# An SSM–MLP forward-and-gradient kernel: main part fused in 512-token chunks, operands turned on chip, up-projections in halves

## The chip, the cores and the metric

The kernel runs on one core of a Trainium2 chip. The metric is device time in microseconds (us), lower is better; several executions are taken of each kernel, and each execution is marked fast or slow. Comparisons are made between fast ones. Engines are named as in the profile: PE multiplies matrices (PEld loads its stationary operand), DVE works on vectors, ACT evaluates functions and scales, POOL and SP mostly issue transfers in this kernel.

## The reference, cut to what matters

Two long-convolution layers alternate with two MLPs, and everything is differentiated:

```python
x = A_q                                     # 2048 tokens x 448, bf16
x = x + A(layernorm(x))                     # A(n) = n * y,  y = fftconv(shift(k) * v, ssm_k) + D * kv
x = x + silu(layernorm(x) @ w1) @ w2        # 448 -> 1792 -> 448
x = x + A(layernorm(x))                     # the same y
x = x + silu(layernorm(x) @ w1) @ w2
out, vjp = jax.vjp(...)                     # 9 outputs: out and the gradients of
                                            # q, k, v, shift_k, ssm_k, D, w1, w2
```

`y` is the same for both layers. So the work falls into a **prefix** (FFT convolution that makes `y`), a **main part** (four residual blocks forward, four backward) and a **suffix** (FFT work of the gradients of k, v, ssm_k). The weight gradients are 896 matmuls that contract over all 2048 tokens; each group of them needs the activations or the up-gradients of a whole layer.

## The kernel before

The main part is a sequence of stages over all tokens. Cuts and shortened lines are marked by dots.

```python
def _forward(k):
    ...                                     # shift product for all 16 token tiles
    _b_forward(k, 0, ...)                   # MLP 0, four chunks of 512 tokens
    for g in range(4): ...                  # layernorm and shift product, all tokens
    _b_forward(k, 1, ...)                   # MLP 1
    for ft in range(NF): ...                # w1 and w2 transposed on PE (112 transposes)

def _b_forward(k, L, ...):
    for c in range(4):
        n_g = _ln_group(...)                # layernorm of this chunk, then 16 transposes
        for fp in range(NF // 2):           # 7 x 8 matmuls, 512 columns
            ...                             # ps_f -> silu, tanh on ACT -> three DVE instructions
        ...                                 # store aT and dT to DRAM
        for tl in range(4): ...             # down-projection, 14 matmuls each, X += ps_o

def _backward(k):
    _b_backward(k, 1, ...); _a_backward(k, 2, ...)
    _b_backward(k, 0, ...); _a_backward(k, 0, ...)   # each _a_backward tile feeds 14 weight-gradient matmuls

class _JFeed:                               # the feeder; one weight-gradient group, cut:
    ...
    nc.sync.dma_start_transpose(out=st[:], in_=stat_d[ft, :, :])     # 512 KB, turned while loading
    for t in range(NT):
        nc.tensor.matmul(ps[:, :D], lhsT=st[:, t, :], rhs=mov[:, t, :], ...)
```

The backward product through w2 contracts 448 rows as four blocks of 112 (`w2T[DC, ND, F]`, DC = 112).

## Time and profile before

| what | value |
|---|---|
| time | 1066.78 us median (1057.07 to 1072.07, 4 runs) |
| PE / DVE / ACT busy in the profiled run (span 1068.9 us) | 808.4 / 653.9 / 391.1 us |
| mean granted PE clock | 0.894 |
| prefix / main / suffix | 176 / 614 / 279 us |

The three parts are read off the table by stage, which the prediction shows. A row has the window, then busy time (and number of instructions) of PE, PEld, DVE, ACT, POOL, the granted clock, the busy share of the 16 transfer engines and GB/s. No engine is full; each stage has another one near its limit, and holes lie at the borders.

### The profile page before, as it was taken

How to read it: one execution, taken by the hardware profiler on the slowest of the kernel's cores; microseconds unless marked ns; L12 is line 12 of the kernel's file. 1: busy time of each engine (PE TensorE's matmuls, PEld its weight loads, DVE VectorE, ACT ScalarE, POOL GpSimd, SP SyncE). 2: the span in 40 equal slices, each digit the busy share in tenths (PEclk: the TensorE clock that was granted, in tenths of full speed). 3: DMA queues.
4: the chain of work that ended last, by engine and by line, in shares of the span. 5: the costliest groups of instructions: out<-in, count | busy, mean ns of one | idle time of the engine just before them, and what ended most of it. 6: DMA issues, size and time to landing. Idle time of an engine off the chain costs nothing.

```text
span 1068.9 us, 12750 instructions
## 1 busy us (share of the span) xinstructions
PE 808.4 (76%) x4908; PEld 429.4 (40%) x4908; DVE 653.9 (61%) x1174; ACT 391.1 (37%) x531; POOL 120.7 (11%) x175
## 2 busy tenths in 40 slices
PE   0676724999699985999977988984737977688387
PEld 0344402444344443444433433431314654445173
DVE  4887738787975562476777866785534663334144
ACT  1768615666566551111233400121213442313112
POOL 1002102111321110000011100010100000102112
PEclk9989976999899995999999989997768988779699
DMA  8516761444436556846799934669789699769945
GB/s 312 196 65 246 237 176 53 168 155 155 172 138 195 179 163 58 230 165 203 240 273 243 251 118 153 218 171 188 148 229 199 184 226 248 226 169 234 163 127 135
DMA packets 173866, 198.00 MB, mean 185 GB/s; under 512 B 121952, under 2 KB 143712, under 8 KB 172525
## 3 DMA queue, kind: packets, MB, share of 16 engines
q1 hardware_dynamic: 151678, 106.56, 41.2%
q0 software_dynamic: 21248, 87.65, 25.0%
q10 hardware_dynamic: 878, 2.98, 0.8%
q8 instruction: 38, 0.62, 0.2%
q14 instruction: 24, 0.19, 0.1%
HBM read 82.59 MB, written 84.87 MB: 157 GB/s over the span
## 4 chain that ended last, share of the span: by engine, by line
issue 43%; PE 15%; POOL 4%; DMA 3%; DVE 2%; ACT 1%; POOLq 0%; DVEq 0%; ACTq 0%
PE ps_f L537 3%; PE ps_d L738 3%; PE ps_o L555 3%; PE ps_b L630 2%; DMA GH_d<-ghT 1%; PE ps_gK L856 1%; DMA out_dram<-dout 1%; PE ps_w2t L512 1%; POOL GH_d L633 1%; POOL W1TP_d L696 1%; PE ps_w1t L505 1%; DMA out_dram<-gk 1%; DMA dstat<-GH_d 1%; POOL W2P_d L696 1%; POOL out_dram L709 1%
## 5 line engine op out<-in xcount | busy, mean ns | idle before, releaser
L738 PE MATMUL ps_d<-dmov,dstat 128*128 128x448 bf16 x896 | 210.5, 387 | 54.9 <-DMA dstat<-GH_d 30.6
L738 PEld LDWEIGHTS <-dstat 128*128 128x128 bf16 x896 | 91.6, 106 | 150.2 <-issue 37.9
L630 PE MATMUL ps_b<-gT,w2T 112*128 112x512 bf16 x448 | 108.4, 389 | 12.0 <-DVE ghT L631 11.9
L537 PE MATMUL ps_f<-nT,w1sb 112*128 112x512 bf16 x448 | 108.9, 391 | 9.5 <-DVE nT L114 8.4
L631 DVE SCALAR_TENSOR_TENSOR ghT<-dTl,ps_b 128x512 bf16<-128x512 bf16 x112 | 75.9, 685 | 37.0 <-PE ps_b L630 26.5
L555 PE MATMUL ps_o<-w2sb,aT 128*128 128x448 bf16 x448 | 91.5, 353 | 1.0 <-ACT aT L539 1.0
L639 PE MATMUL ps_n<-w1T,ghT 128*128 128x448 bf16 x448 | 88.8, 354 | 0.0
L568 DVE SCALAR_TENSOR_TENSOR lb_junk<-lb_u,nch 128x448 bf16<-128x448 f32 x64 | 39.8, 622 | 66.1 <-ACT lb_u L565 66.0
L565 ACT ACTIVATE lb_u<-ps_n,rhalf 128x448 f32<-128x448 f32 x32 | 20.3, 635 | 163.2 <-issue 125.3
L630 PEld LDWEIGHTS <-w2T 112*128 112x128 bf16 x448 | 44.2, 99 | 71.2 <-issue 27.5
L537 PEld LDWEIGHTS <-w1sb 112*128 112x128 bf16 x448 | 44.5, 100 | 67.3 <-issue 23.3
L539 ACT ACTIVATE aT<-ps_f 128x1024 bf16<-128x1024 f32 x56 | 58.1, 1038 | 11.6 <-PE ps_f L537 7.5
L272 PE MATMUL ps_v<-Gsb,pa 128*128 128x128 bf16 x336 | 48.0, 231 | 18.6 <-DVE pa L812 16.0
L639 PEld LDWEIGHTS <-ghT 128*128 128x128 bf16 x448 | 44.0, 98 | 42.6 <-issue 1.1
L555 PEld LDWEIGHTS <-aT 128*128 128x128 bf16 x448 | 42.5, 98 | 46.1 <-ACT aT L539 6.7
L541 ACT ACTIVATE tm<-ps_f 128x1024 bf16<-128x1024 f32 x56 | 58.2, 1040 | 0.0
L447 ACT ACTIVATE n_g<-X,ln_nmr,rstd 128x448 bf16<-128x448 f32 x41 | 30.1, 770 | 67.1 <-DVE ln_nmr L441 43.8
L112 ACT COPY dpart<-ps_d 128x448 f32<-128x448 f32 x28 | 14.9, 532 | 97.4 <-PE ps_d L738 90.1
L273 PE MATMUL ps_v<-Gsb,pb 128*128 128x128 bf16 x336 | 44.8, 232 | 5.2 <-DVE pb L406 4.6
L272 PEld LDWEIGHTS <-pa 128*128 128x128 bf16 x336 | 34.9, 104 | 25.5 <-DVE pa L812 19.7
L572 DVE SCALAR_TENSOR_TENSOR lb_v<-nch,lb_cc,lb_u 128x448 f32<-128x448 bf16 x64 | 43.6, 682 | 1.0
L525 PE MATMUL ps_nt<-ident,n_g 128*112 128x128 bf16 x128 | 12.2, 245 | 40.8 <-ACT n_g L447 40.8
(173 smaller groups left out, 1244.2 us busy)
## 6 DMA issues: line engine op xcount, KB each, us to landing
A_d<-aT POOLq DMA_DIRECT2D x8, 1792.0 KB, 8.2
DT_d<-dT POOLq DMA_DIRECT2D x8, 1792.0 KB, 10.3
dTl<-DT_d SPq DMA_DIRECT2D x8, 1792.0 KB, 12.8
GH_d<-ghT POOLq DMA_DIRECT2D x8, 1792.0 KB, 12.7
N_d<-n_g POOLq DMA_DIRECT2D x16, 448.0 KB, 3.8
nch<-N_d SPq DMA_DIRECT2D x16, 448.0 KB, 5.0
spec_K<-Ka POOLq DMA_DIRECT2D x2, 1792.0 KB, 7.8
kbc<-spec_K SPq DMA_DIRECT2D x14, 256.0 KB, 5.1
```

Source lines behind the costliest of these rows:

```text
L272: nc.tensor.matmul(pv[:, i, :], lhsT=pa[:, i * P:(i + 1) * P], rhs=k.Gsb[:, ga, :], start=True, stop=False)
L273: nc.tensor.matmul(pv[:, i, :], lhsT=pb[:, i * P:(i + 1) * P], rhs=k.Gsb[:, gb, :], start=False, stop=True)
L537: nc.tensor.matmul(ps[:, u, :], lhsT=w1sb[:, dc, ft * P:(ft + 1) * P], rhs=nT[:, dc, :], start=(dc == 0), stop=(dc == ND - 1))
L539: nc.scalar.activation(asl, ps[:], ACT.Silu)
L541: nc.scalar.activation(tm[:], ps[:], ACT.Tanh, scale=-0.5)
L555: nc.tensor.matmul(po[:, :D], lhsT=aT[:, ft, tl * P:(tl + 1) * P], rhs=w2sb[:, ft, :], start=(ft == 0), stop=(ft == NF - 1))
L568: nc.vector.scalar_tensor_tensor(out=junk[:], in0=u0[:], scalar=1.0, in1=n_t, op0=ALU.mult, op1=ALU.mult, accum_out=cpair[:, 1:2])
L572: nc.vector.scalar_tensor_tensor(out=v[:], in0=n_t, scalar=cc[:, 1:2], in1=u0[:], op0=ALU.mult, op1=ALU.add)
L630: nc.tensor.matmul(ps[:], lhsT=w2T[:, dc, ft * P:(ft + 1) * P], rhs=gT[:, dc, :], start=(dc == 0), stop=(dc == ND - 1))
L631: nc.vector.scalar_tensor_tensor(out=ghT[:, ft, :], in0=dT[:, ft, :], scalar=1.0, in1=ps[:], op0=ALU.add, op1=ALU.mult)
L639: nc.tensor.matmul(pn[:, :D], lhsT=ghT[:, ft, tl * P:(tl + 1) * P], rhs=w1T[:, ft, :], start=(ft == 0), stop=(ft == NF - 1))
L738: nc.tensor.matmul(ps[:, :D], lhsT=st[:, t, :], rhs=mov[:, t, :], start=(t == 0), stop=(t == NT - 1))
```

## The change

Its intent is to overlap the stages. A chunk of 512 tokens goes through shift, layernorm, MLP and, in layer 1, backward at once, while the next chunk's shift and layernorm are prepared; the up-projection is written in two halves so that one half of the next chunk comes between. Further parts: constants come ready as bf16; the shift convolution moves from DVE to PE; weight-gradient operands are turned by a transfer from SBUF to SBUF and stored turned; w1 and w2 are transposed by transfers. The suffix swaps one spectrum instead of two, and the feeder is gone: the weight gradients are low-priority instructions that the scheduler places. The diff is cut to its core; dots mark cuts and shortened arguments.

```diff
-    k.A_d = [... [NF, P, S] ...]             # loads turn
+    k.A_d = [... [P, NF, NT, P] ...]         # stored turned
+    def store_turned(self, dst, tile_, c, hh):
+        an = self.td.tile([P, NF // 2, 4, P], BF16, name="turned", tag="S", bufs=2)
+        nc.sync.dma_start_transpose(out=an, in_=tile_)
+        nc.gpsimd.dma_start(out=dst[:, 7 * hh:7 * hh + 7, 4 * c:4 * c + 4, :], in_=an[:])
...
+    def run(self):
+        for c in range(4):                                  # layer 0 forward
+            ...a_fwd(c + 1), nb = b_pre(c + 1)              # next chunk's shift, layernorms
+            self.h(c, 0, nT, 1, cur)                        # second half of this up-projection
+            nT = self.b_tr(nb)
+            self.h((c + 1) % 4, 0 if c < 3 else 1, nT, 0, fol)   # first half of the next
+            self.out(c, cur, False)
+        for c in range(4):                                  # layer 1, forward and backward
+            gb, gT = self.g_pre(c, 1)
+            self.h(c, 1, nT, 1, cur)
+            na1, nb1 = self.a_fwd(c + 1, 2, None), self.b_pre(c + 1, 3)
+            self.out(c, cur, True)
+            ghT = self.ga(c, 1, gT, cur)
+            nT = self.b_tr(nb1); self.h(c + 1, 1, nT, 0, cur)
+            self.gn(c, 1, ghT, nb, ...)
+        for c in range(4):                                  # layer 0 backward
+            ghT = self.ga(c, 0, gT, dT); ...; self.gn(c, 0, ghT, nb, ...)
...
-    nc.tensor.matmul(ps[:], lhsT=w2T[:, dc, ...], rhs=gT[:, dc, :], ...)          # 4 blocks of 112 rows
+    r0 = 64 if b == 3 else 0
+    nc.tensor.matmul(ps[:, u, :], lhsT=self.w2T[r0:P, b, ...], rhs=gT[r0:P, b, :], ...)   # 128, 128, 128, 64
```

## The prediction

> **What bounds the kernel now.** I read the engine totals first, then the 40 slices, the busy time stage by stage, the costliest groups, and last the DMA issues of one line.
>
> No engine is full over the run: PE 808.4 us of 1068.9 (76%), DVE 653.9 (61%), ACT 391.1 (37%). The slices show why:
>
> ```profile
> PE   0676724999699985999977988984737977688387
> ...
> DVE  4887738787975562476777866785534663334144
> ...
> PEclk9989976999899995999999989997768988779699
> ```
>
> PE is at 9 only where an MLP runs, and DVE is low exactly there. The table by stage (window, then busy time and instructions of each engine, granted clock, DMA share, GB/s) makes it exact:
>
> ```profile
> 0.00:25.00 25.00, 0.13 (x2) 0.13 (x3) 11.54 (x13) 3.18 (x2) 3.76 (x11) 1.00 0.87 313
> 25.00:104.00 79.00, 53.23 (x418) 32.49 (x418) 65.24 (x102) 57.93 (x69) 9.11 (x13) 0.96 0.47 172
> ...
> 141.00:176.00 35.00, 2.77 (x17) 2.03 (x18) 20.80 (x37) 4.05 (x7) 2.59 (x3) 0.56 0.50 151
> 176.00:280.00 104.00, 98.67 (x496) 46.30 (x494) 83.11 (x159) 69.30 (x80) 17.63 (x19) 0.98 0.42 145
> 280.00:302.00 22.00, 11.89 (x50) 5.80 (x51) 19.83 (x59) 12.93 (x17) 8.62 (x8) 0.69 0.51 183
> 302.00:396.00 94.00, 90.16 (x468) 43.13 (x467) 59.77 (x101) 55.30 (x60) 11.64 (x14) 1.00 0.53 167
> 396.00:433.00 37.00, 21.53 (x140) 14.93 (x140) 7.39 (x21) 5.80 (x11) 0.51 (x1) 0.54 0.75 128
> ...
> 710.00:790.00 80.00, 46.43 (x177) 20.02 (x177) 43.34 (x79) 14.92 (x38) 8.11 (x15) 0.79 0.80 168
> 790.00:844.00 54.00, 37.84 (x242) 20.53 (x243) 21.77 (x28) 14.33 (x15) 3.24 (x6) 0.81 0.81 204
> ```
>
> Three gaps: nothing on PE before 24.9 us; 35 us at 141 with PE at 2.77 (the first shift and layernorm, for all tokens, before any MLP); 37 us at 396 with DVE at 7.4 (weights being transposed). The first `ps_f` starts at 176 us, the suffix at about 790. So I split the run as **prefix 176, main 614, suffix 279**.
>
> Groups (busy, mean ns, idle before and what ended it):
>
> ```profile
> L738 PE MATMUL ps_d<-dmov,dstat 128*128 128x448 bf16 x896 | 210.5, 387 | 54.9 <-DMA dstat<-GH_d 30.6
> L568 DVE SCALAR_TENSOR_TENSOR lb_junk<-lb_u,nch 128x448 bf16<-128x448 f32 x64 | 39.8, 622 | 66.1 <-ACT lb_u L565 66.0
> L525 PE MATMUL ps_nt<-ident,n_g 128*112 128x128 bf16 x128 | 12.2, 245 | 40.8 <-ACT n_g L447 40.8
> ```
>
> The weight gradients (`ps_d`) wait for their transposed operand, the layernorm backward on DVE waits for ACT, and a new MLP's transposes wait for layernorm: all stage boundaries. Mean ns of pipelined matmuls overlap; by their starts, fed ones come 55 to 56 ns apart at 128 columns, 189 to 192 at 448 and 220 to 227 at 512. The transposing loads hold the SP queue:
>
> ```profile
> L734 SPq DMA_TRANSPOSE dstat<-A_d x28: 1318/4154/9980, 395.2 to 910.3; - x28
> ```
>
> (minimum/median/maximum ns; those of `GH_d` have median 2642.) A plain load's issue takes SP 300 to 600 ns.
>
> **What the Trainium skill says.**
> - "TensorE: Matmul & The Clock Gate", Part 2, Back-to-back issue gap: about N/2.4 + 2.5 ns when warm, 56 for 128 columns, 216 for 512. The trace agrees (55 to 56; 220 to 227).
> - "VectorE: DVE Perf Modes", The TRN2 errata, and Why PSUM operands drop a tier: fp32 and PSUM operands go one element a cycle, (N+151)/0.96 ns. 448 gives 624; the trace's `lb_junk` has 622. bf16 two-operand work runs at twice that; 1024 gives 690, the trace 685.
> - "Advanced Engine Details and Errata", X-Bar Transpose (TRN2): transpose DMAs are as fast as regular ones. The trace agrees for landing (512 KB in 6.3 us median, plain ones 4.7 to 5.8), not for the issuing queue, which is held for microseconds.
> - "Perfetto Trace Analysis", Optimization Strategy: interleave stages whose most contended engines differ. The table above is such a case: 302:396 is PE, 280:302 DVE.
>
> **The change part by part.** Little arithmetic goes away, so I price stages.
>
> *Floor.* PE's work in the changed kernel (its instruction order has as many rows, 9626 against 9818), at fed spacings, is about 713 us. ACT rises to about 436 us (391 before), DVE is about 639 (654 before). The gain must come from overlap.
>
> *Prefix.* bf16 constants and a stored inverse matrix take the casts and 64 transposes off the start: I put the first PE work at about 7 us instead of 24.9. The shift convolution leaves DVE (28 ops of 128x1792, 35 us) for 256 matmuls of 112 columns, 256 x 0.056 = 14 us. The spectra product is software-pipelined. The step to inverse output (`ps_y`) ended at 141; less 18 for the start and some 15 of the 35 us (the rest lay beside ACT's casts) gives about 107. Then only chunk 0 has to be shifted and normalised, about 10 us instead of 35. First up-projection at **117** (176 before): 59 gained.
>
> *Main.* DVE per 512-token chunk, by durations of before's rows:
> - Up-projection: 7 pairs x (0.44 + 0.69 + 0.69) = 12.75 (silu and its derivative). Residual 4 x 0.616 = 2.5. Two layernorms 2 x 4 x (0.60 + 0.17), with small ops 6.8. Shift products 3.1. Layer 0 forward: **25.1**.
> - Fused layer 1 adds `ghT` 7 x 1.22 = 8.5 (from PSUM), eight layernorm backwards at .622 + .082 + .165 + .682 + .681 = 2.23 = 17.9, and gradient products 5.0: **56.5**.
> - Layer 0 backward: 8.5 + 17.9 + 7.4 = **33.8**.
>
> Four of each: 100 + 226 + 135 = **461 us on DVE**. PE per chunk forward: 56 up-projection matmuls x 0.222 = 12.4, 56 down x 0.191 = 10.7, 16 transposes x 0.056 = 0.9, 24 in all; backward has the same counts (`ps_b`, `ps_n`); a fused chunk has both, 48. Four of each: 4 x 96 = **386 us**, and 227 `ps_d` x 0.19 = 43 more that main still holds (below): 429. I checked the forward figure: the last forward chunks of before come every 25.2 us. DVE therefore becomes the bound of main, where before PE was (302:396: PE 90 of 94). The order also shows only 227 of 896 `ps_d` before the end of main, against about 453 before. DVE runs in order and per token tile waits for ACT's scaled copy of PSUM about 0.35 to 0.4 us, x64 = 24, and there are chunk ends: I add 7%. Main **about 490** (614 before).
>
> *Moved with it.* 24 turns on chip (128x3584, 917 KB) take the place of 42 of the 56 transposing loads. They sit on SP, beside work, two per half chunk. The 112 PE transposes of w1 and w2 go, and with them the 37 us hole at 396. One partial sum (`W1TP`) stored and reloaded goes too.
>
> *Suffix.* Now 669 `ps_d` are left instead of 443. Terms: gY's first stages and turns 22; product of 7 pairs at about 10.3 = 72 (PE: before's 844:934 took 90 for it, at DMA share 1.01, now without the swapped loads); gK 14, gkv 10, shift-kernel gradient 12, gk about 14; the last 448 `ps_d` alone, 448 x 0.195 = 88; stores 6. Sum **238** (279 before). The 226 more matmuls cost 43 us; dropped transposes, wide instead of narrow matmuls and relieved transfers pay for them.
>
> Sum: 117 + 490 + 238 = **845**; I say **850**, as waits are more often forgotten than invented.
>
> **The rivals.**
> - *The SP queue bounds main.* A turned tile is 1.75 times a loaded one; scaling the held times of 2.6 to 4.15 us by that gives an estimated 5 to 7 us and perhaps 9. A fused chunk has four: 20 to 36 us of 57. For it: other loads and stores on that queue stand behind, only three buffers hold operands. Against: it fits the chunk. If each turned tile held up its next user, +20 us a fused chunk: 930.
> - *DVE's waits are not hidden.* Its chain per token tile is serial with ACT's, and `lb_junk` already waited 66 us. If main stays 20% over its DVE work: 555, total 910.
> - *The end is a tail of weight gradients on PE alone.* Counted above. If it is fed slowly (each group of 32 needs two or more 512 KB operands; 6.3 us landings, DMA share already 1.05 in before's 975:1018) it takes 110 rather than 88: 870.
> - *Everything overlaps.* Prefix 110, main 477, suffix 225: 812.
>
> **Range and chances.** Best case 812, less some error in the suffix: 800. A bad one is half of one of the first two rivals plus the slow tail, 910. To be within 2% of 1065 it would have to lose every gain but 21 us, which needs two rivals in full together. Faster 0.97, within 2% 0.02, slower 0.01.
>
> **What would show it.** Right: first PE work near 7 us, first up-projection (`ps_h`) near 117; main ending near 605; DVE over 85% busy in the fused layer-1 stretch with PE near 80%; a solid stretch of the last 448 `ps_d` with PE at 9 and DVE almost idle, about 88 us; no slice of clock near 0.55 in the middle. Wrong: transposes in the SP queue holding it over 7 us, with PE or DVE groups waiting for turned operands (first rival); DVE under 80% in that stretch and `lb_junk` again waiting for ACT (second); `ps_d` waiting for DMA at the end (third). The prediction is wrong altogether if main does not drop below 540, or if the prefix still reaches 140.

## The result, and the profile after

The changed kernel takes **879.88 us** (median; 874.28 to 890.23, 4 runs, one of them slow; 878.35 is the median of the fast ones) against 1066.78 before. The ratio is 0.8239, 95% interval 0.8153 to 0.8325. PE is busy for 776.9 of 879.5 us (88%), DVE for 582.2, ACT for 390.4. The slices of the changed kernel's page:

```profile
PE   6888699689999999999998988888788995989997
...
DVE  4498877588866979979698987882474743650100
...
PEclk9899889989999999999999999998899997999999
```

PE works from the first slice, no slice of clock near 0.55 is left, and DVE is busy beside PE up to slice 27. The last four slices are PE alone. The table by stage of the changed kernel, cut at the first `ps_h`, the first `ps_g` (backward of layer 1), the start of layer 0's backward, the end of the main part, the end of the spectra product, and the end of the k gradient:

```profile
0.00:109.00 109.00, 83.98 (x915) 63.04 (x921) 77.60 (x140) 73.38 (x88) 28.10 (x54) 0.95 0.97 277
109.00:251.00 142.00, 128.67 (x639) 60.02 (x639) 111.09 (x253) 103.98 (x132) 31.61 (x39) 0.94 0.94 243
251.00:443.00 192.00, 182.41 (x898) 78.44 (x907) 155.89 (x315) 93.49 (x139) 22.94 (x29) 1.00 0.71 188
443.00:604.00 161.00, 144.47 (x673) 60.50 (x680) 133.48 (x271) 39.92 (x93) 17.86 (x26) 0.97 0.64 208
604.00:713.00 109.00, 91.03 (x815) 58.51 (x821) 58.41 (x83) 49.93 (x52) 9.67 (x17) 0.94 0.81 256
713.00:790.00 77.00, 62.27 (x380) 36.00 (x379) 37.12 (x93) 20.71 (x24) 17.99 (x31) 0.89 0.84 223
790.00:880.00 90.00, 84.04 (x472) 42.95 (x469) 8.61 (x14) 8.99 (x15) 10.48 (x15) 0.98 0.64 155
```

So prefix, main part and suffix are 109, 495 and 275 us, against 176, 614 and 279. **Of the 190 us between these two profiled runs, 67 are won in front and 119 in the main part; the suffix as a whole gave 4.** The group that the prediction led with, and the transposing transfers (the turned tile and the remaining turning loads; minimum/median/maximum ns on SP):

```profile
L731 PE MATMUL ps_d<-dmov,dstat 128*128 128x448 bf16 x896 | 190.9, 359 | 16.1 <-DMA dstat<-A_d 13.1
...
L473 SPq DMA_TRANSPOSE turned<-aT x16: 4107/4278/7912, 120.9 to 405.8; - x16
...
L711 SPq DMA_TRANSPOSE dstat<-GH_d x14: 1322/1934/10212, 724.2 to 860.8; - x14
```

`ps_d` waits 16.1 us instead of 54.9. A turn of 917 KB holds SP for 4.28 us, less than the 5 to 7 estimated.

### The profile page after: what moved, and what is told of

The parts are those of the page before. It is cut to its first block, busy times and chain, and to the rows that moved or that the text cites. A ratio compares the mean times of both kernels' runs of the same rounds, so it can differ in the third digit from the quotient of the medians.

```text
span 879.5 us, 12450 instructions
## 1 busy us (share of the span) xinstructions
PE 776.9 (88%) x4783; PEld 399.5 (45%) x4812; DVE 582.2 (66%) x1166; ACT 390.4 (44%) x539; POOL 138.7 (16%) x209
## 4 chain that ended last, share of the span: by engine, by line
issue 43%; DVE 13%; DMA 8%; PE 7%; POOL 6%; ACT 3%; POOLq 0%; DVEq 0%; ACTq 0%; SPq 0%
PE ps_g L582 4%; DMA turned<-ghT 3%; DMA turned<-aT 3%; PE ps_o L551 2%; DMA out_dram<-gK 2%; DVE w1p L537 2%; DVE dT L538 2%; DVE X L603 1%; DVE lb_junk L599 1%; DVE lb_u L602 1%; DVE w1p L536 1%; POOL out_dram L768 1%; PE ps_h L528 1%; POOL W2P_d L741 1%; POOL GH_d L593 1%
## 5 line engine op out<-in xcount | busy, mean ns | idle before, releaser
L731 PE MATMUL ps_d<-dmov,dstat 128*128 128x448 bf16 x896 | 190.9, 359 | 16.1 <-DMA dstat<-A_d 13.1
L582 PE MATMUL ps_g<-gT,w2T 128*128 128x512 bf16 (+1 forms) x430 | 120.3, 383 | 3.4 <-DVE ghT L585 1.9
L528 PE MATMUL ps_h<-nT,w1sb 112*128 112x512 bf16 x448 | 108.8, 391 | 7.4 <-ACT dT L533 6.0
L582 PEld LDWEIGHTS <-w2T 128*128 128x128 bf16 x448 | 36.0, 96 | 87.0 <-issue 67.3
L532 ACT ACTIVATE aT<-ps_h 128x1024 bf16<-128x1024 f32 (+1 forms) x64 | 59.0, 922 | 17.8 <-issue 9.5
L533 ACT ACTIVATE dT<-ps_h 128x1024 bf16<-128x1024 f32 (+1 forms) x64 | 59.2, 925 | 0.0
L585 DVE SCALAR_TENSOR_TENSOR ghT<-dT,ps_g 128x1024 bf16<-128x1024 bf16 (+1 forms) x32 | 34.2, 1078 | 11.7 <-PE ps_g L582 11.5
L537 DVE TENSOR_TENSOR w1p<-w1p,aT 128x1024 bf16<-128x1024 bf16 (+1 forms) x64 | 39.6, 618 | 0.9
L538 DVE TENSOR_TENSOR dT<-w1p,dT 128x1024 bf16<-128x1024 bf16 (+1 forms) x64 | 39.5, 617 | 0.8
L238 PEld LDWEIGHTS <-pb 128*128 128x128 bf16 x336 | 33.1, 100 | 13.2 <-DVE pb L826 4.6
L585 DVE SCALAR_TENSOR_TENSOR ghT<-dTl,ps_g 128x1024 bf16<-128x1024 bf16 (+1 forms) x32 | 34.6, 1082 | 5.0 <-PE ps_g L582 5.0
```

Source lines behind the costliest of these rows:

```text
L238: nc.tensor.matmul(pv[:, i, :], lhsT=pb[:, i * P:(i + 1) * P], rhs=k.Gsb[:, gb, :], start=False, stop=True)
L528: nc.tensor.matmul(ps[:, u, :], lhsT=self.w1sb[:, dc, ft * P:(ft + 1) * P], rhs=nT[:DC, dc, :], start=(dc == 0), stop=(dc == ND - 1))
L532: nc.scalar.activation(a, ps[:, 0:n, :], ACT.Silu)
L533: nc.scalar.activation(tm, ps[:, 0:n, :], ACT.Tanh, scale=-0.5)
L537: nc.vector.tensor_tensor(out=wv, in0=wv, in1=a, op=ALU.mult)
L538: nc.vector.tensor_tensor(out=tm, in0=wv, in1=tm, op=ALU.subtract)
```

## The experiments

Every kernel below is the changed kernel with the edit shown. All gave right results except the one that is wrong on purpose. Medians are of all runs; slow runs are in four of them (one each of changed, no_wgrad and full_rows, two of wgrad_main_64). Differences are between medians of the fast runs alone, against 878.35. The ratios to the kernel before, taken on the same chip, are the check.

| kernel | median us | difference | ratio to before, 95% interval |
|---|---|---|---|
| changed | 879.88 | | 0.8239 (0.8153 to 0.8325) |
| chunk_by_chunk | 1007.97 | +130 | 0.9467 (0.9398 to 0.9535) |
| whole_up | 923.34 | +45 | 0.8655 (0.8587 to 0.8722) |
| shift_all_first | 912.13 | +34 | 0.8544 (0.8492 to 0.8597) |
| turn_on_load | 900.74 | +22 | 0.8479 (0.8427 to 0.8532) |
| dve_extra | 891.46 | +13 | 0.8396 (0.8323 to 0.8469) |
| pe_extra | 928.97 | +51 | 0.8739 (0.8687 to 0.8791) |
| no_wgrad | 755.94 | -123 | 0.7069 (0.7013 to 0.7125) |
| full_rows | 884.58 | +5 | 0.8256 (0.8176 to 0.8335) |
| store_sp | 876.59 | -2 | 0.8204 (0.8150 to 0.8258) |
| wgrad_main_64 | 872.72 | -13 | 0.8199 (0.8088 to 0.8310) |
| wgrad_main | 860.50 | -18 | 0.8071 (0.8021 to 0.8122) |
| all_four | 848.00 | -30 | 0.7942 (0.7903 to 0.7982) |

The record calls wgrad_main_64 unclear, with two fast runs of four. The means of the fast runs that it lists give a ratio of 0.812, not the 0.8199 recorded.

### What bounds the main part: more work on one engine

Two probes add about 40 us of work each to the backward halves of the main part.

```diff
 # dve_extra, in ln_bwd
         nc.vector.scalar_tensor_tensor(out=junk[:], in0=u0, ..., accum_out=cp[:, 1:2])
+        nc.vector.scalar_tensor_tensor(out=junk[:], in0=u0, ..., accum_out=cp[:, 1:2])
 # pe_extra, in gn
-            for ft in range(NF):
+            for ft in (*range(NF), *range(NF)) if tl % 2 else range(NF):
                 nc.tensor.matmul(pn[:, :D], lhsT=ghT[ft // 7]..., start=(ft == 0), stop=(ft == NF - 1))
```

> The changed kernel with the product-and-sum instruction of each layernorm backward issued twice: 64 more DVE instructions of 128x448, 64 x 0.62 = 40 us more DVE work, all between 285 and 603 us, where DVE is 82% busy and PE 93%. Same result. Theory D (DVE bounds the main part, as predicted): about +36 us, 916. Theory P (PE bounds it, as its busy share of 93 to 95% there suggests): under +12 us, 880 to 892. Theory L (neither; a serial chain through PE, DVE and ACT inside each chunk bounds it): +20 to +40 from this, and the same from the PE probe.

> The changed kernel with half of the down-gradient groups (ps_n, every second token tile) computed twice into the same PSUM tile: 32 / 2 x 14 = 224 more matmuls of 448 columns, at 0.19 us fed, 43 us more PE work in the same stretch as the DVE probe. Same result. Theory D: under +12 us, 880 to 892. Theory P: about +40 us, 920. Theory L: +20 to +40, like the DVE probe.

By the total, theory P comes nearest: +13 for DVE (its interval just meets the changed kernel's), +51 for PE. The traces say more. The last `gYb`, some 6 us before the main part's end, in the changed kernel, with more DVE work, and with more PE work (the last two numbers ahead of the semicolon are the first and last start in us):

```profile
L628 DVE TENSOR_TENSOR gYb<-gy,gyt x16: 615/618/626, 474.2 to 597.3; 128x448 bf16<-128x448 f32 x16
```

```profile
L629 DVE TENSOR_TENSOR gYb<-gy,gyt x16: 616/618/626, 493.5 to 624.8; 128x448 bf16<-128x448 f32 x16
```

```profile
L628 DVE TENSOR_TENSOR gYb<-gy,gyt x16: 614/618/627, 488.0 to 603.1; 128x448 bf16<-128x448 f32 x16
```

More DVE work ends the main part 27.5 us later, more PE work only 5.8. What differs is the filler. In PE's order the changed kernel has 122 weight-gradient matmuls before the last `ps_n`; with more DVE work it has 197, with more PE work 5. The main part stretched by DVE takes in 75 matmuls (75 x 0.189 = 14 us) that then need not run later; the PE work pushes 117 of them (22 us) out, and they come back behind the main part. These 22 us are half of the 43 by which the way from there to the last stretch grew; of the rest, a wait of `ps_sk` for DVE grew from 1.1 to 13.8 us, and why was not followed. **So the end of the main part moves more with DVE's work than with PE's, and the total more with PE's, because the weight gradients are moved about by whatever room is left.**

DVE's work is not all that sets this end, and the added instruction also lengthens the serial chain of DVE and ACT in each token tile; these two were not told apart. From the first `gYb` to the last, the changed kernel takes 123.1 us and the DVE probe 131.3, but the PE probe only 115.1 and the version with most weight gradients left out (`no_wgrad`, below) 116.8, with the same DVE work. So less filler went with a shorter layer 0's backward, and filler placed by hand (below) shortens it too. Why is open: PE's waits for the filler's operands before the last `ps_n` are 3.0 us in all. Within the fused stretch the two are near balance: the last `ps_h`, four fifths into it, came 13.5 us later for some 15 us of added DVE work and 17.1 us later for 16 us of added PE work (403.0, 416.5 and 420.1 us). There theory L, a chain through both, fits best, by one trace each.

### What the interleaving is worth

```diff
 # chunk_by_chunk: all of a chunk before the next
-            self.a_fwd(c + 1, ...); nb = self.b_pre(c + 1, 1)
-            self.h(c, 0, nT, 1, cur); nT = self.b_tr(nb)
-            self.h((c + 1) % 4, ..., 0, fol)
-            self.out(c, cur, False)
+            self.h(c, 0, nT, 0, cur); self.h(c, 0, nT, 1, cur); self.out(c, cur, False)
+            self.a_fwd(c + 1, ...); nb = self.b_pre(c + 1, 1); nT = self.b_tr(nb)
 # (layer 1 likewise, its backward ahead of the next chunk's shift)
 # whole_up: next chunk's layernorm still prepared, up-projection not halved
-            self.h((c + 1) % 4, ..., 0, fol)      # after the next chunk's transposes
+            self.h(c, 0, nT, 0, cur)              # at the chunk's own start
```

> The changed kernel with the neighbouring chunks taken apart: every chunk's shift, layernorm, up-projection, down-projection and (layer 1) backward are written one after the other before the next chunk begins; sizes and counts unchanged. Theory: interleaving is what fills the main part, so each of 8 chunk boundaries gets a hole of a layernorm chain (two layernorms, shift products, transposes: 8 to 11 us): +60 to +90 us, 940 to 970. Rival: the scheduler and the other engines' slack hide it, the fusion in chunks alone is the gain: under +20 us.

> The changed kernel without halves: each chunk's up-projection is written whole ahead of its own down-projection; the next chunk's shift, layernorms and transposes are still written ahead of it, as in the changed kernel. Theory: the interleaving is worth 128 us (chunk by chunk ran at 1008) and most of it comes from the prepared layernorm; the halves alone give what PE waits for silu and its product at each of 8 chunk starts, 2 to 4 us each: +15 to +35 us, 895 to 915. Rival: the halves are the larger share, over +60 us.

Chunk by chunk takes 1008 us, more than expected. Its last `gYb` stands at 719.7 us instead of 597.3, so the main part is back at the length it had before the change. Fusing in chunks alone gives nothing there; the interleaving is the gain. The waits in its main part show where (us in total, times, longest):

```profile
PE ps_t L490 <- ACT nb L279: 81.4, 12, 26.9
```

The transposes of the next chunk wait for its layernorm, 81 us in all. In the changed kernel's main part the same wait is 5.3 us. The granted clock over this run, with PE idle more often, was 0.905, against 0.96.

The halves alone are worth 45 us, above the 15 to 35 expected. Without them PE meets these waits in the main part, of which the changed kernel has 0.6, 1.9 and 6.0 us:

```profile
PE ps_o L551 <- ACT aT L532: 17.9, 8, 10.3
PE ps_g L582 <- DVE ghT L585: 16.6, 2, 9.3
PE ps_o L551 <- DVE X L552: 11.3, 6, 5.4
```

A whole up-projection is followed by products that need its last silu; a half of another chunk in between covers it.

### The first shift and layernorm as a stage

```diff
+            for c in range(1, 4):
+                self.a_fwd(c, 0, self.x0_load(c))       # ahead of the first up-projection
...
-                self.a_fwd(c + 1, 0, self.x0_load(c + 1))
```

> The changed kernel with layer 0's first layernorm and shift products of all four chunks written ahead of the first up-projection, as a stage of its own (the kernel before did this for all tokens). It moves 3 chunks x (3.1 + 3.4) = about 20 us of DVE work from the main part to in front of it. If PE bounds the forward part, the start slips and nothing is won back: first ps_h at about 127 to 130 instead of 109, total +12 to +20 us. If DVE bounds the forward part, what slips in front is saved behind: total within 4 us.

The first `ps_h` came at 138.8 us, 29.6 later where 18 to 21 were expected, and almost nothing was won back: the last `gYb` stood at 625.9, 28.6 later. So shifting one chunk only ahead of the first MLP is about 30 of the prefix's 67 us. It also shows that the forward part is not bound by DVE. Its chunks start 25.5 us apart where nothing disturbs them, near the 23.6 us that PE needs for one (56 x 0.216 + 56 x 0.189 + 16 x 0.056).

### Turning on chip or on load

```diff
 # turn_on_load
-        nc.sync.dma_start_transpose(out=an, in_=tile_); nc.gpsimd.dma_start(out=dst[...], in_=an[:])
+        nc.gpsimd.dma_start(out=dst[7 * hh:7 * hh + 7, :, 512 * c:512 * (c + 1)]..., in_=tile_[:])
...
-        k.nc.sync.dma_start(out=st[:], in_=src[:, ft, :, :])
+    k.nc.sync.dma_start_transpose(out=st[:], in_=src[ft, :, :])      # all 56
```

> The changed kernel with the turning on chip undone: the activations and up-gradients are stored as they are and all 56 weight-gradient operands are transposed by their loads, as in the kernel before. Theory 1 (turning on chip costs main nothing and feeds the weight gradients better at the end): +10 to +30 us, ps_d waiting for its operand again and the last stretch of ps_d longer than 89 us. Theory 2 (24 turns of 4.3 us on the SP queue hold main up): main shorter, total -5 to -20 us. Theory 3: it moves nothing, within 5 us.

Theory 1 holds in the total, +22 us, but not in all its steps. The turns do cost the main part something: without them the last `gYb` stands at 591.4, 6 us earlier. The loss comes later: gK's first matmul (`ps_gK`) starts at 729.8 us instead of 713.2. `ps_d` waits longer for its activations (over the whole run, first without, then with turning on chip):

```profile
PE ps_d L726 <- DMA dstat<-A_d: 26.1, 6, 6.5
```

```profile
PE ps_d L731 <- DMA dstat<-A_d: 13.1, 7, 4.1
```

Of these 26.1 us, 13.3 lie between 598 and 730, against 5.5 in the same stretch of the changed kernel; so this wait is about a third of the loss there, and the rest was not followed. The last stretch, from the first `ps_dt` to the last, is 84.0 us in both; I had expected it longer.

### The share of the weight gradients that lies bare

```diff
 # no_wgrad: wrong on purpose
-    for ft in range(NF):
+    for ft in range(1):
```

> The changed kernel with one of 14 column groups of each weight-gradient job only: 64 of the 896 ps_d matmuls, so 832 x 0.19 = 158 us of PE work gone, and the weight gradients wrong on purpose. Theory: the last 416 of them stand alone (79 us) and the 102 after the main part too (19 us); the others are half hidden: total 110 to 135 us less, 745 to 770. Rival 1: PE bounds everywhere, 158 us less, 720. Rival 2: only the tail is exposed, about 85 less, 795.

Taking 832 matmuls away (157 us at 0.189) gives 123 us, as expected. Four fifths of the weight gradients' time is not hidden; 34 us of it is. The two weight gradients came out wrong (not all their columns are written).

### Switching rows in ps_g

PE's records showed a cost that the instruction counts had not. In the fed stretches half of the `ps_g` start 311 ns after the one before, not 216, always where the contraction goes from 128 rows to 64 or back.

```diff
 # full_rows
+        nc.gpsimd.memset(self.w2T[0:64, 3, :], 0.0)
-                    r0 = 64 if b == 3 else 0
+                    r0 = 0
```

> The changed kernel cuts the contraction of w2's backward product (ps_g) into blocks of 128, 128, 128 and 64 rows where the kernel before had four of 112. By their starts, half of its matmuls now come 311 ns apart instead of 216, always at a switch between 128 and 64 rows. Here the fourth block is 128 rows too, 64 of them zeros, so no switch is left; counts and order on PE stay the same. Theory P (PE bounds the backward part; the switch costs it): 112 groups x 2 switches x 0.096 = 21 us less, 858 to 862, and spacing 216 throughout. Theory D (DVE bounds): within 5 us of the changed kernel, about 878. Rival on the cause: the spacing of 311 comes from waits for DVE or PSUM, not from the rows, and stays.

The cause is confirmed: 24 matmuls in a row of the changed kernel, then of this one (start and length in us of the run of instructions):

```profile
317.19 6.49 PE L582 MATMUL ps_g<-gT,w2T 128*128 128x512 bf16 x24 [0.35 <-DVE ghT L585]
```

```profile
318.14 5.68 PE L583 MATMUL ps_g<-gT,w2T 128*128 128x512 bf16 x24
```

No spacing of 311 is left and PE's busy time fell from 776.9 to 764.9 us, and yet the time did not fall (fast medians 883.15 against 878.35; the intervals of the ratios overlap almost wholly). The last `gYb` stands at 596.9, as before. This is the number of theory D. That the order on PE, where each weight-gradient matmul has its fixed place, could not use what was freed is my reading; the next section tries another order.

### A store that holds a layernorm up

The changed kernel's forward chunks start at 109.2, 136.6, 162.1, 195.7 and 221.1 us: one takes 33.6 instead of 25.5. In it PE waits 5.29 us for ACT (start, length, and in brackets the idle time before):

```profile
176.79 3.57 PE L528 MATMUL ps_h<-nT,w1sb 112*128 112x512 bf16 x8 [5.29 <-ACT dT L533]
```

POOL's rows just ahead show the cause:

```profile
171.93 0.95 POOL L474 DMA_DIRECT2D A_d<-turned  x1 [10.55 <-DMA turned<-aT]
172.90 1.03 POOL L272 TENSOR_TENSOR rstd<-ln_ve,mhalf 128x4 f32<-128x4 f32 x1
```

POOL waits 10.55 us for a turn to land before it may issue its store, and the layernorm's 1-us power instruction stands behind it.

```diff
 # store_sp
-        nc.gpsimd.dma_start(out=dst[:, 7 * hh:7 * hh + 7, ...], in_=an[:])
+        nc.sync.dma_start(out=dst[:, 7 * hh:7 * hh + 7, ...], in_=an[:])
```

> The changed kernel with the store of each turned tile issued on SP, behind its own turn, instead of on POOL. In the changed kernel POOL, which takes its instructions in order, waits 112 us for turns to land ahead of these stores, and the layernorm's power instruction (rstd) stands behind it: DVE waits 27 us for rstd in all, once 8.7 us, and one forward chunk takes 34 us instead of 25. Theory: with POOL free of that wait the forward chunk of 34 us falls to 25 or 26, the first ps_g comes at 243 instead of 251, the main part ends near 588 and the total is 8 to 12 us less, 868 to 872. Rival 1: the turns themselves land late because the 16 transfer engines are full (share 0.97 to 1.04 there), and SP, now waiting for landings, holds later loads: no gain or a loss of up to 10. Rival 2: the main part ends earlier, but as the order of the weight gradients is fixed they do not move up and the gain is only half.

In its trace the long chunk is gone (its chunks start 23.8 to 25.6 us apart): the first `ps_g` starts at 238.3 us instead of 251.4, the last `gYb` at 587.7 instead of 597.3, and the profiled span is 870.6 instead of 879.5. DVE's wait for `rstd` in the main part falls from 27.2 to 9.9 us. The mechanism is shown. The gain in time is not settled by these runs: 870.05 to 881.0 us against 874.28 to 881.4, and the intervals of the ratios overlap.

### Filling the main part by hand, and a better version

```diff
 # wgrad_main: full_rows, and one weight-gradient group written into each token tile of layer 0's backward
-    with tc.issue_after(k.d0_load.ins):
-        _wgrad_w2_first(k)
...
             for ft in range(NF): ...            # ps_n
+            if fill is not None:
+                next(fill, None)                # 16 ps_d
 # wgrad_main_64: the same without full_rows
 # all_four: wgrad_main, store_sp, and the gK stores on ACT's queue
-            nc.gpsimd.dma_start(out=out5v[:, dc, :], in_=gK[:])
+            nc.scalar.dma_start(out=out5v[:, dc, :], in_=gK[:])
```

> The version with full rows in ps_g (no 64-row block), and the first weight-gradient job written into layer 0's backward, one group of 16 ps_d per token tile, instead of as low-priority filler: in PE's order 178 ps_d now stand before the last ps_n instead of 125, and 48 instead of 102 between the main part and the suffix. Theory (DVE bounds the end of the main part, PE's freed 20 us was left idle because the order of ps_d was fixed): the main part ends as before, near 600, and the 53 moved ps_d take 10 us off what follows: 865 to 872. Rival: PE has no room in the backward part, the main part ends 10 us later, total as before, 878 to 886.

> The version with the first weight-gradient job written into layer 0's backward, but with the 64-row block of the changed kernel kept in ps_g; PE's order is instruction for instruction that of the version with full rows, which ran at 860. Alone, full rows gave nothing (884 against 880). Theory: with the weight gradients filled in, PE's 21 us of switches now lie where PE has no slack left, so this runs 10 to 20 us slower than 860: 870 to 880. Rival: DVE bounds the main part all the same and moving the weight gradients was the whole gain: 857 to 865.

> Four edits together, as a try for a better version: full rows in ps_g, first weight-gradient job inside layer 0's backward, turned tiles stored from SP, and the stores of gK issued on ACT so that they do not queue behind 5.5 MB of loads on POOL's queue (in the changed kernel ACT waits 16.6 us for one of them). If the gains add: 10 + 10 + 8 us, 850 to 858. If PE's total work bounds the end and moved holes are only refilled: about 868. If SP becomes the bound by waiting: 880 or more.

With the weight gradients written into the backward, 176 of them stand before the last `ps_n` instead of 122, and the run takes 860.50 us. The interval lies clear of the changed kernel's. The main part did not end as before but earlier: last `gYb` at 582.2, 14.7 us before full rows alone, with the same DVE work. So PE's order moves this end too, which neither theory had (one trace each). With the 64-row block kept, in the same order, it is at 590.1. Two of that version's four runs were slow; its fast ones, 863.38 and 868.14, lie below the 870 to 880 of the theory and at the upper edge of the rival's 857 to 865, and the intervals overlap. How the 18 us divide between the order and the rows is open.

All four edits together take **848.00 us** (844.18 to 854.33, 6 runs), 3.6% less than the changed kernel by the ratios (0.7942 / 0.8239 = 0.964). That is below the 850 to 858 expected if the gains add; as the gK stores were not tried alone, what each edit gave is not split. gK's wait for an earlier store is 4.4 us instead of 16.6, the main part ends near 577, and what follows takes 266 us instead of 275.

## Why the prediction was right, and where it was not

The time, 850 with a range of 800 to 910, held: 880. By its own steps:

- **Prefix, 117 predicted, 109 measured.** First PE work at 4.93 us (7 predicted); the last `ps_y` starts at 102.0 and lands near 102 (107); 7 us from there to the first `ps_h` (10). That one chunk's shift instead of all gave about 30 us is shown by undoing it. That the convolution on PE gave its share is only argued; it was not undone.
- **Main part, 490 predicted, 495 measured, but not by the working given.** The DVE sum was 461: 126 for the stretch up to the first `ps_g`, which holds five chunks' forward, 201 for the fused stretch (three forward, four backward), 135 for layer 0's backward. These stretches took 142, 192 and 161 us with DVE busy for 111, 156 and 133: 400 us, not 461. **The term that was mis-sized is DVE's work, because durations were added.** In the trace consecutive DVE records overlap: one that lasts 0.62 us is followed by the next after 0.54. Over the 838 records of the main part the durations add up to 452 us and the busy time is 400. The idle time was then too small by as much: 95 us, where the 7% came to some 30. The two errors cancelled, so that main came out right was luck. The floor's DVE (639) and ACT (436) were too high as well: 582.2 and 390.4 us were measured.

```profile
451.84 0.62 DVE L624 TENSOR_TENSOR gyt<-X,na 128x448 bf16<-128x448 f32 x1
452.38 0.62 DVE L630 TENSOR_TENSOR lb_u<-X,Ysb 128x448 f32<-128x448 f32 x1
452.91 1.21 DVE L585 SCALAR_TENSOR_TENSOR ghT<-dTl,ps_g 128x1024 bf16<-128x1024 bf16 x1
```

- **"DVE becomes the bound of main" is half right.** The end in layer 0's backward moves with DVE's work more than with PE's, but also with the order of the filler; the fused stretch answers to both engines (DVE 81% busy there and PE 95%, where DVE over 85% and PE near 80% were predicted); the forward follows PE and one stalled chunk.
- **PE's work was under-sized.** "Backward has the same counts" was true, but 112 groups of `ps_g` switch rows twice at 0.096 us, by that count 21 us in all. Taking the switches out gave nothing by itself; with the weight gradients written in, the main part ended 7.9 us earlier without them (one trace each).
- **Suffix, 238 predicted, 275 measured: the largest miss of a term.** The product (71 against 72), gkv with the shift gradient (24 against 22) and the last stretch (89 against 88 plus stores of 6) were right. First stage and turns took 38 instead of 22: the 102 weight-gradient matmuls behind the last `ps_n` were all credited to the main part, but the last 32 of them are left at 604, and with two waits for their operands (3.0 us) they stand in front of the suffix's first matmul, which starts at 615.1. They are not the whole delay: the load of that matmul's constants (`M1s`) is issued at 604.3 only, and with hardly any weight gradients (`no_wgrad`) the matmul came 4.9 us after that issue. gK took 27 instead of 14, with one wait of 16.6 us in which ACT waits for the store of an earlier gK tile. The k gradient took 26 instead of 14; which of its waits is to blame was not tried.
- **The rivals.** The SP queue did not bind: 4.28 us a turn (one took 14.3), and undoing the turns ends the main part only 6 us earlier. What did hold a chunk up was one step on, in POOL's queue, which no rival named. DVE's unhidden waits did come (95 us of the main part's time), made up by the smaller work; `lb_junk`, though, waited only 21.5 us for ACT, not 66. The tail was fed at full rate: 84 us, `ps_d` back to back.
- **Readings of the trace before that do not hold.** "DVE is low exactly there" fits layer 1's forward (59.77 of 94 us) and not layer 0's, where DVE was busy for 83.11 of 104 us beside PE. By their starts most 512-column matmuls came 215 to 216 ns apart there too, not 220 to 227. The 28 shift instructions add up to 30.6 us, not 35, and 4 x 96 is 384, not 386. (On the page cited for the issue gap, see the last section.)
- **Where the expected gain of overlap went.** PE's busy time fell by 31 us only and its idle time from 260 to 103; the clock rose from 0.894 to 0.96. The rest of what PE could give lies in the tail, where 448 weight-gradient matmuls run with DVE almost idle, and removing all weight-gradient matmuls but 64 shows 123 us bare.

## What to carry to other kernels

When stages with different limits are overlapped, cost the filler too: with work that can be moved about, the end of a stage and the total can have different bounds, and a probe must be read at both places. Where the filler stands in the order matters as well as how much of it there is: written in by hand, it gave 18 us together with the full rows. Interleaving with the next chunk was the gain here (130 us of the total, 45 of them by the halves), chunking alone none. Look behind any instruction that waits on a queue for what else that queue carries: a 1-us layernorm step stood behind a store that waited 10.55 us.

## What the Trainium skill lacked or had wrong

- "TensorE: Matmul & The Clock Gate", Part 2, Back-to-back issue gap, gives the formula that the prediction uses for a single matmul alone, and 81 and 131 ns for streams of 128 and 512 columns. The streams here came at 55 to 56 and 215 to 216 ns from start to start, as the formula has it.
- "VectorE: DVE Perf Modes", The DRAIN you can't avoid, says that the next instruction does not start until the pipe empties, and adds that one that is not held starts earlier. Here the second is the common case: records 0.62 us long follow each other after 0.54 us, and 838 records of 452 us take 400 us of DVE.
- "TensorEngine Tiling (Array Packing)", Key Properties, says that a change of tiling mode drains TensorE, and gives no cost. If a block of 64 rows is such a change, this is its size: going from 128 to 64 contraction rows or back took 0.096 us here (311 instead of 216 ns from start to start, 512 columns).
- "Advanced Engine Details and Errata", X-Bar Transpose (TRN2): transposing transfers are as fast as regular ones. They landed as fast here (512 KB in 4.5 us median, plain loads in 4.8), but held the issuing queue for 4.28 us per 917 KB from SBUF to SBUF, and 1.9 to 4.2 us (medians) per 512 KB from DRAM, where a plain load's issue took 0.32 us.
- "Perfetto Trace Analysis", Optimization Strategies, says that PE should be kept busy, but not that PE's busy share can be high (95% in the fused stretch) while 12 us less of it (full_rows) changes nothing clear of noise.
- No page that I read gives, beside the order of the queues, the case of a store on POOL that waits for another transfer and so holds POOL's own computing instructions: 10.55 us once, for one instruction of 1.03 us.
